# The last unit of a fused recommender kernel: a transpose in halves, three stores on the GpSimd queue, one fused VectorE operation

## The chip, the cores and the metric

The kernel runs on one core of one Trainium2 chip. The metric is device time in microseconds (us), the median over repeated runs. Each kernel also has a profile of one execution, whose span, from the first to the last instruction, is some 2 us shorter than the time (2275.2 of 2277.03 us in the profiled run of the kernel before).

## The reference

Six layers of a cross network on 16384 rows of 1024 features, in bf16:

```python
def reference(x0, ws, bs):
    x = x0                                  # 16384 x 1024
    for l in range(ws.shape[0]):            # 6 layers
        proj = jnp.einsum('bd,de->be', x, ws[l]) + bs[l]
        x = x0 * proj + x
    return x
```

## The kernel before

The kernel works on pairs of blocks of 512 rows, feature by feature on the partitions, so x is transposed. There are 16 pairs and 6 layers, hence 96 units, each a Strassen-like product with four result blocks Q, U, V and W. The last unit has code of its own, because its result must be transposed back and stored while no later work hides it:

- Q (block 11) and U (block 12) go through a DMA transpose on the sync queue and then through a store;
- V (block 22) and W (block 21) are transposed on TensorE against an identity into PSUM, copied to SBUF by ScalarE and VectorE, and stored in halves.

A table of ranks orders the last unit's operations; each engine's queue follows it.

```python
RLAST = {**R0, **ranks("""
...
trQ@19 stQ@24 trU@22.5 stU@26 stVa@27 stVb@27.5 stWa@28 stWb@29
""")}
...
            for m in range(KH):
                ttop(f"Wm{m}", W[:, m, :], W[:, m, :], blk(x0T, 1, 0)[:, m, :], MULT, ...)
            for nm, n in (("Q", 0), ("U", 1)):
                def tr(n=n, xfin=xfin, xo=xo):
                    nc.sync.dma_start_transpose(out=xo[:, 0, n]..., in_=xfin[:, 0, n]...)
                add("tr" + nm, tr, [f"xf{nm}0", f"xf{nm}1"] + XT, [f"xo{nm}"])

                def st(n=n, xo=xo, r0=r0):
                    nc.sync.dma_start(out[r0 + n * NB:r0 + (n + 1) * NB, 0:H]..., xo[:, 0, n]...)
                add("st" + nm, st, [f"xo{nm}"], ["out"])
            for nm, C, bank, n in (("V", V, pX, 1), ("W", W, pA, 0)):
                for m in range(KH):
                    ...                       # transposes on TensorE into PSUM
                    def cp(...):
                        if nm == "V" or m == 3:
                            nc.scalar.copy(out=d, in_=s_)
                        else:
                            nc.vector.tensor_copy(out=d, in_=s_)
```

## Time and profile before

| | kernel before |
|---|---|
| time, median of the first 3 runs | 2277.72 us (2276.81 to 2277.87) |
| TensorE busy | 2265.4 of 2275.2 us |
| last transposing matmul starts | 2269.19 us |
| last copy ends | 2270.08 us |
| last store issued, landed | 2270.16, 2273.92 us |
| end of the span | 2275.25 us |

Issues, ends and landings are single records of the trace; a landing is the last of the 16 semaphore updates of a transfer. The lines themselves stand in the prediction below.

### The profile page before, as it was taken

The page shows a single profiled execution, that of the slowest core. Times are in us where ns is not written, and L with a number is a line of the kernel's source. Part 1 is how long each engine was busy: PE and PEld are TensorE (multiplying, and loading weights), DVE is VectorE, ACT ScalarE, POOL GpSimd, SP SyncE. Part 2 cuts the span into 40 slices and gives each one's busy share as a digit, 9 for nine tenths or more (in the row PEclk, how much of TensorE's full clock was granted, in tenths as well). Part 3 has the DMA queues.
Part 4 walks back from the last instruction along what each step waited for, and adds up shares of the span by engine and source line. Part 5 has one row for each costly group of instructions (what it writes and reads, how often), then busy time and mean ns, then how long its engine had stood idle before and what let it go on. Part 6 is the DMA issues. An engine that isn't in the chain of part 4 may idle for free.

```text
span 2275.2 us, 34978 instructions
## 1 busy us (share of the span) xinstructions
PE 2265.4 (100%) x12951; PEld 1264.0 (56%) x12951; DVE 2079.9 (91%) x2326; ACT 1839.4 (81%) x3228; POOL 22.1 (1%) x43
## 2 busy tenths in 40 slices
PE   9999999999999999999999999999999999999998
PEld 4455555555555555555555555555555555555554
DVE  7999999999999999999999999999999999999997
ACT  5678888888888888888888888888888888888887
POOL 1110000000000000000000000000000000000000
PEclk9999999999999999999999999999999999999999
DMA  9779797796977969779697796978969689696872
GB/s 279 229 270 289 261 242 269 219 301 209 252 257 221 288 217 260 250 226 283 213 274 241 228 283 204 273 245 230 283 200 292 226 232 286 194 303 216 241 240 65
DMA packets 625868, 557.01 MB, mean 245 GB/s; under 512 B 397600, under 2 KB 552224, under 8 KB 625696
## 3 DMA queue, kind: packets, MB, share of 16 engines
q1 hardware_dynamic: 618864, 534.58, 79.1%
q0 software_dynamic: 5184, 18.88, 2.2%
q8 instruction: 101, 1.65, 0.3%
q10 hardware_dynamic: 1648, 1.32, 0.2%
q14 instruction: 71, 0.58, 0.1%
HBM read 436.22 MB, written 52.43 MB: 215 GB/s over the span
## 4 chain that ended last, share of the span: by engine, by line
PE 98%; DVE 1%; SPq 0%; DMA 0%; issue 0%; ACT 0%; DVEq 0%
PE pA L285 57%; PE pX L389 24%; PE pX L285 16%; DVE ev L198 1%; SPq L529 0%; DMA wp<-in_ws_dram 0%; DVE xst L198 0%; DVE T L198 0%; DVE ti L198 0%; DVE wp L198 0%; SPq L538 0%; ACT ev L294 0%; DVE x0T L487 0%; DVEq L608 0%; DVEq L198 0%
## 5 line engine op out<-in xcount | busy, mean ns | idle before, releaser
L285 PEld LDWEIGHTS <-wp 128*128 128x128 bf16 x7904 | 772.3, 98 | 843.7 <-issue 3.9
L285 PE MATMUL pA<-T,wp 128*128 128x512 bf16 x4608 | 1054.9, 379 | 0.5 <-DVE T L198 0.5
L294 ACT ACTIVATE ev<-pA,b_all 128x512 bf16<-128x512 f32 x1124 | 704.8, 690 | 211.8 <-PE pA L285 211.4
L389 PEld LDWEIGHTS <-wp 128*128 128x128 bf16 x4984 | 487.1, 98 | 156.6 <-issue 15.2
L198 DVE TENSOR_TENSOR ev<-ev,x0T 128x2048 bf16<-128x2048 bf16 (+2 forms) x484 | 482.7, 999 | 8.1 <-ACT ev L294 1.5
L198 DVE TENSOR_TENSOR xst<-ev,xst 128x2048 bf16<-128x2048 bf16 x319 | 388.9, 1219 | 18.6 <-DVE ev L198 0.5
L389 PE MATMUL pX<-ti,wp 128*128 128x256 bf16 x2848 | 397.6, 272 | 0.0
L198 DVE TENSOR_TENSOR ev<-ev,ev 128x2048 bf16<-128x2048 bf16 (+1 forms) x283 | 343.7, 1215 | 26.7 <-ACT ev L294 9.8
L294 ACT ACTIVATE ev<-pX,b_all 128x512 bf16<-128x512 f32 x412 | 289.4, 705 | 59.9 <-PE pX L285 49.3
L285 PE MATMUL pX<-xst,wp 128*128 128x512 bf16 x1376 | 336.4, 379 | 0.0
L285 PE MATMUL pA<-xst,wp 128*128 128x512 bf16 x1280 | 313.5, 379 | 0.0
L290 ACT COPY pX<-pA 128x512 f32<-128x512 f32 x412 | 256.3, 625 | 44.7 <-PE pA L285 44.3
L290 ACT CAST ev<-pX 128x512 bf16<-128x512 f32 x384 | 224.8, 619 | 49.0 <-ACT ev L294 37.6
L198 DVE TENSOR_TENSOR ev<-iu,ip 128x1024 bf16<-128x1024 bf16 x178 | 122.4, 688 | 120.7 <-ACT iu L290 120.7
L290 ACT COPY pX<-pX 128x512 f32<-128x512 f32 x356 | 208.7, 587 | 8.4
L290 ACT CAST iu<-pX 128x512 bf16<-128x512 f32 x356 | 196.8, 639 | 0.0
L198 DVE TENSOR_TENSOR T<-xst 128x2048 bf16<-128x2048 bf16 x160 | 194.8, 1217 | 0.3
L198 DVE TENSOR_TENSOR T<-xst,T 128x2048 bf16<-128x2048 bf16 x160 | 194.5, 1216 | 0.0
L389 PE MATMUL pX<-T,wp 128*128 128x256 bf16 x1068 | 160.2, 273 | 0.0
L290 ACT CAST ip<-pX 128x512 bf16<-128x512 f32 x178 | 104.7, 589 | 54.1 <-PE pX L389 54.1
L389 PE MATMUL pX<-xst,wp 128*128 128x256 bf16 x888 | 133.2, 273 | 0.0
L198 DVE TENSOR_TENSOR xst<-ev,x0T 128x2048 bf16<-128x2048 bf16 x64 | 78.2, 1222 | 1.6
(44 smaller groups left out, 624.3 us busy)
## 6 DMA issues: line engine op xcount, KB each, us to landing
wp<-Lc SPq DMA_DIRECT2D x538, 512.0 KB, 4.6
wp<-in_ws_dram SPq DMA_DIRECT2D x285, 512.0 KB, 5.3
out_dram<-x0T SPq DMA_DIRECT2D x30, 1024.0 KB, 8.6
Lc<-wp POOLq DMA_DIRECT2D x24, 512.0 KB, 6.2
Lc<-isum POOLq DMA_DIRECT2D x12, 512.0 KB, 6.9
w<-in_ws_dram SPq DMA_DIRECT2D x5, 512.0 KB, 6.3
wp<-in_ws_dram ACTq DMA_DIRECT2D x2, 512.0 KB, 5.8
out_dram<-x0T SPq DMA_DIRECT2D x2, 512.0 KB, 3.6
```

Source lines behind the costliest of these rows:

```text
L198: nc.vector.tensor_tensor(out=o, in0=a, in1=b, op=op)
L285: nc.tensor.matmul(bank[:], lhsT=wt[(u, w)][:, k, m * P:(m + 1) * P], rhs=rhs[:, k, :], start=(start and k == 0), stop=(k == KH - 1), skip ...
L290: add(name, lambda: nc.scalar.copy(out=dst, in_=src), rd, wr)
L294: add(name, lambda: nc.scalar.activation(out=dst, in_=src, func=IDENT, bias=b_all[:, c:c + 1], scale=1.0), rd, wr)
L389: nc.tensor.matmul(pX[bank][:, m * NQ:(m + 1) * NQ], lhsT=wv[:, k, m * P:(m + 1) * P], rhs=rhs[:, k, :], start=(start and m == 0 and k == ...
```

## The change

Its intent is a shorter tail. The U transpose is cut in two, so that its first half need not wait for the second half of U. The stores of Q and U leave the sync queue, where they stand behind transposes, for the GpSimd queue. The last quarter of W is biased and multiplied in one VectorE operation straight from PSUM, which frees ScalarE of its last activation, and the copies of W are dealt out anew.

```diff
-trQ@19 stQ@24 trU@22.5 stU@26 stVa@27 stVb@27.5 stWa@28 stWb@29
+trQ@19 stQ@20 trU0@20.5 trU1@22.5 stU0@24 stU1@26 stVa@27 stVb@27.5 stWa@28 stWb@29
...
-            biased(f"E4.{m}", W[:, m, :], pA[m][:], 1, m, [A[m]], [f"W.{m}"])
+            if not (last and m == KH - 1):
+                biased(f"E4.{m}", W[:, m, :], pA[m][:], 1, m, [A[m]], [f"W.{m}"])
...
-            for m in range(KH):
+            for m in range(KH - 1):
                 ttop(f"Wm{m}", W[:, m, :], W[:, m, :], blk(x0T, 1, 0)[:, m, :], MULT, ...)
...
+            add("Wm3", lambda c=c, x0T=x0T: nc.vector.scalar_tensor_tensor(
+                out=W[:, KH - 1, :], in0=pA[KH - 1][:], scalar=b_all[:, c:c + 1],
+                in1=blk(x0T, 1, 0)[:, KH - 1, :], op0=ADD, op1=MULT), ...)
+            outs = [("Q", xfin[:, 0, 0], xo[:, 0, 0], 0, 0, H)]
+            outs += [(f"U{h}", xfU[:, h], xoU[:, h], NB, h * HQ, (h + 1) * HQ) for h in range(2)]
+            for nm, src, dst, r, c0, c1 in outs:
+                add("tr" + nm, lambda ...: nc.sync.dma_start_transpose(...), ...)
+                add("st" + nm, lambda ...: nc.gpsimd.dma_start(...), ["xo" + nm], ["out"])
...
-                        if nm == "V" or m == 3:
+                        if nm == "V" or m in (0, 2):
                             nc.scalar.copy(out=d, in_=s_)
```

More of the change, by code (lines that the diff above doesn't have):

```diff
@@ L440 @@
             xfin, xo = quad(xsts[free]), quad(x0Ts[free])
+            halves = lambda t: t[:].rearrange("r n k (j p) -> r (n k j) p", p=P)[:, KH * KH:2 * KH * KH].rearrange(
+                "r (h j k) p -> r h j k p", h=2, j=KH)
+            xfU, xoU = halves(xsts[free]), halves(x0Ts[free])
             XF = [f"xs.{free}.{a}{b}" for a, b in QD]
@@ L455 @@
                 ttop(f"Vx{h}", V[:, sl], V[:, sl], blk(xs, 1, 1)[:, sl], ADD, half("V", h) + [XI[1, 1]], half("V", h))
-                ttop(f"Ux{h}", xfin[:, 0, 1].rearrange("r j k p -> r k j p")[:, sl], v4(U[:])[:, sl],
+                ttop(f"Ux{h}", xfU[:, h].rearrange("r j k p -> r k j p"), v4(U[:])[:, sl],
                      v4(blk(xs, 0, 1))[:, sl], ADD, half("U", h) + [XI[0, 1]] + XF, [f"xfU{h}"])
-            for m in range(KH):
+            for m in range(KH - 1):
                 ttop(f"Wm{m}", W[:, m, :], W[:, m, :], blk(x0T, 1, 0)[:, m, :], MULT, [f"W.{m}", X0[1, 0]], [f"W.{m}"])
-            for nm, n in (("Q", 0), ("U", 1)):
-                def tr(n=n, xfin=xfin, xo=xo):
-                    nc.sync.dma_start_transpose(out=xo[:, 0, n].rearrange("p j k r -> p (j k) r"),
-                                                in_=xfin[:, 0, n].rearrange("r j k p -> r (j k p)"))
-                add("tr" + nm, tr, [f"xf{nm}0", f"xf{nm}1"] + XT, [f"xo{nm}"])
-                def st(n=n, xo=xo, r0=r0):
-                    nc.sync.dma_start(out[r0 + n * NB:r0 + (n + 1) * NB, 0:H].rearrange("(j p) d -> p j d", p=P),
-                                      xo[:, 0, n].rearrange("p j k r -> p j (k r)"))
-                add("st" + nm, st, [f"xo{nm}"], ["out"])
@@ new lines @@
+            c = l * KD + 2 * KH - 1
+            add("Wm3", lambda c=c, x0T=x0T: nc.vector.scalar_tensor_tensor(
+                out=W[:, KH - 1, :], in0=pA[KH - 1][:], scalar=b_all[:, c:c + 1], in1=blk(x0T, 1, 0)[:, KH - 1, :], op0=ADD, op1=MULT),
+                [A[KH - 1], X0[1, 0]], [f"W.{KH - 1}"])
+            outs = [("Q", xfin[:, 0, 0], xo[:, 0, 0], 0, 0, H)]
+            outs += [(f"U{h}", xfU[:, h], xoU[:, h], NB, h * HQ, (h + 1) * HQ) for h in range(2)]
+            for nm, src, dst, r, c0, c1 in outs:
+                add("tr" + nm, lambda src=src, dst=dst: nc.sync.dma_start_transpose(
+                    out=dst.rearrange("p j k r -> p (j k) r"), in_=src.rearrange("r j k p -> r (j k p)")),
+                    (["xfQ0", "xfQ1"] if nm == "Q" else ["xf" + nm]) + XT, ["xo" + nm])
+                add("st" + nm, lambda dst=dst, r=r0 + r, c0=c0, c1=c1: nc.gpsimd.dma_start(
+                    out[r:r + NB, c0:c1].rearrange("(j p) d -> p j d", p=P), dst.rearrange("p j k r -> p j (k r)")),
+                    ["xo" + nm], ["out"])
```

## The prediction

> **What bounds the kernel now.** I read the page first, then the last 20 us of the trace, since the diff touches only the last of 96 units. The head of the page and its chain say that the matmuls bind the whole program:
>
> ```profile
> span 2275.2 us, 34978 instructions
> PE 2265.4 (100%) x12951; PEld 1264.0 (56%) x12951; DVE 2079.9 (91%) x2326; ACT 1839.4 (81%) x3228; POOL 22.1 (1%) x43
> ```
>
> TensorE is busy for 2265.4 of 2275.2 us, and no matmul is removed. So only the few us in which TensorE no longer sets the pace can change. The timeline of the sync engine in the tail (start, length of the issue, both in us) shows the order in which transfers leave:
>
> ```profile
> 2254.48 1.82 SPq L462 DMA_TRANSPOSE x0T<-xst  x1
> ...
> 2262.86 1.32 SPq L462 DMA_TRANSPOSE x0T<-xst  x1
> ...
> 2264.28 1.25 SPq L467 DMA_DIRECT2D out_dram<-x0T  x1
> ...
> 2267.24 0.38 SPq L467 DMA_DIRECT2D out_dram<-x0T  x1
> ...
> 2268.22 0.37 SPq L491 DMA_DIRECT2D out_dram<-x0T  x1
> ...
> 2269.20 0.98 SPq L491 DMA_DIRECT2D out_dram<-x0T  x2
> ```
>
> The first transpose (block 11, "Q") has landed by 2258.94 (the trace's landing record), but its store leaves at 2264.28: it stands on the same queue behind the second transpose (block 12, "U"), which waits for VectorE until 2262.86. The view of DMA activity from 2254 to 2274 (40 slices of 0.5 us, busy tenths, then GB/s) shows what that costs:
>
> ```profile
> DMA  0005999940000000000089999999799999999980
> GB/s 0 0 0 117 214 214 218 203 101 0 0 0 0 0 0 0 0 0 0 0 180 211 215 211 207 351 375 320 240 346 336 294 296 255 286 289 285 292 252 3
> ```
>
> The DMA engines idle from 2258.7 to 2264.3 and are then full until 2273.7. The waits of the sync engine and the two last instructions of the other engines complete the picture:
>
> ```profile
> SPq L608 <- DMA out_dram<-x0T: 3.7, 1, 3.7
> ```
>
> ```profile
> 2269.44 0.58 ACT L485 CAST x0T<-pA 128x512 bf16<-128x512 f32 x1 [0.27 <-PE pA L476]
> 2270.16 0.39 ACTq L491 DMA_DIRECT2D out_dram<-x0T  x1
> ```
>
> Compute ends at 2270.1; the last store is issued at 2270.16 and lands at 2273.92; a fixed closing sequence of 1.3 us follows (2275.2 - 2273.9). The end is therefore a queue of stores, and not the last evictions.
>
> **What the Trainium skill says.** "DMA: Bandwidth & Descriptors", section "Issuing engines are not separate DMA queues": all issuers share 16 DMA engines, and another issuer saves only issue time. The GpSimd queue thus adds no bandwidth; it only removes the wait behind the transpose. The trace agrees that the data share the engines: one store from ScalarE and four from the sync engine land one after another (2270.25, 2271.13, 2272.12, 2273.39, 2273.92).
> The same page, "Latency and other measured facts", puts the first byte at about 1 us for the GpSimd path and 0.6 us for the hardware path. Here the undisturbed GpSimd stores at the start of the program moved their first packet 1.10 to 1.25 us after issue (at 33.86, 68.59, 102.57 and 115.48), and the hardware store issued at 2267.24 about 1.07 us after (2268.3). So the penalty of the GpSimd path is small in this trace when it is undisturbed.
> "SBUF — State Buffer", section "SBUF: two separate sides", warns that VectorE in a 2-port mode keeps GpSimd from writing descriptors. VectorE runs without a pause from 2258.63 to 2270.1, in two-input operations. The trace is ambiguous: the store issued at 115.48 had its first data at 1.14 us under a running VectorE, but others, with loads in flight too, took 3 to 6 us (82.40, 152.06).
> "VectorE: DVE Perf Modes", section "The perf-mode tier table": a two-input operation with a PSUM operand runs at 1x. The trace's PSUM casts of 128x512 take 680 ns on VectorE against 418 ns for the bf16 product that the fused operation replaces.
>
> **The change, part by part.**
> (1) Store of block 11 to the GpSimd queue. It can leave at 2258.97, has data from 2260.1 and is done by about 2261.6, in the idle gap. In the kernel before it moved between 2266.5 and 2268.2; these 1.7 us of DMA time leave the full stretch.
> (2) Block 12 in two halves. VectorE finishes the first half at 2260.09 + 0.69 = 2260.78, so its transpose leaves about 2260.8. A transpose has data 1.47 us after issue (2262.86 to 2264.33) and moves some 213 GB/s: 0.262 MB in 1.23 us, landed about 2263.7. Its store leaves then, from GpSimd, and moves from 2264.8. The second half's transpose still leaves at 2262.86, moves from 2264.3, shares the engines with that store and lands by about 2266.4; its store has data from about 2267.6 and is done at 2268.5 to 2269.5, as 0.262 MB takes 0.9 us at the 290 GB/s of the last stretch.
> (3) The fused last result. One ScalarE activation (687 ns) of the last unit disappears. The built programs' order shows it: ScalarE goes straight from its third W activation to the four V copies. The first copy started at 2267.13, right behind that activation; its transposed input is ready about 2266.75, so the V copies come about 0.38 us earlier, the first V store 0.37 us earlier (2267.85 for 2268.22), the second likewise (2268.80). On VectorE the fused operation replaces 0.42 by 0.68 us, ending about 2268.5 instead of 2268.28.
> (4) Copies shuffled: ScalarE takes W 0 and 2, VectorE W 1 and 3. The pair 0 and 1 is ready at 2269.2, so that store goes about 0.4 us earlier. The last pair is set by TensorE: its last transposing matmul starts at 2269.19 in both kernels, because the V products before it wait for VectorE's last V sum (start 2266.25, unchanged). The last copy (680 ns from about 2269.4) ends at 2270.1, and the last store leaves at 2270.16 as before. **Compute gives nothing at the very end**; the gain is in the queue alone.
>
> The sum: in the kernel before the last four stores (1.05 MB) moved from about 2270.0 to 2273.7, 0.93 us each. Now the first of them has data from 2267.85 + 1.07 = 2268.9, and 4 x 0.93 = 3.7 us gives 2272.6, landed 2272.8: **1.1 us earlier** than 2273.92. A floor is the last store alone: 2270.16 + 1.07 + 0.93 + 0.2 for landing = 2272.4, which would be 1.5 us. If half of the second U store still lies behind 2268.9, 0.45 us are lost. I take 0.95 us.
>
> **The rivals.**
> A. *Late descriptors.* The Q and U stores have runs of 1024 and 512 bytes, 512 runs each, where the GpSimd stores seen so far have 128 runs of 4096 bytes. If the descriptors take in proportion longer, or VectorE keeps GpSimd out, the U stores move after 2269 and compete with the V and W stores. One U half behind the line leaves 1.1 - 0.9 = 0.2 us; both make it 0.7 us slower. For it: the store issued at 82.40 waited 6.0 us for its first packet. Against: that was among loads, while here the engines are idle until the second transpose.
> B. *A slow close of the GpSimd queue.* The drain view of the closing line shows a long one:
>
> ```profile
> L608 POOLq DRAIN  x3: 39/93/9104, 162.2 to 2275.0; - x3
> ```
>
> It begins with the last GpSimd store (162.27) and ends at 171.35, 1.5 us after that store landed (169.84). If it follows the landing, the new last GpSimd store (landed about 2269) ends it at 2270.5, long before 2272.8, and it costs nothing. If it were a fixed 9.1 us from the issue (about 2266.5), it would end at 2275.6 instead of the 2274.4 at which the closing sequence began, and the kernel would be 1.2 us slower. I give that one in ten.
> C. *Nothing visible.* The three runs before spread over 1.06 us (2276.81 to 2277.87), as much as the gain; the profile of one execution could show a shorter tail with equal medians.
>
> **Range and chances.** The mean of the three runs before is 2277.5 (their median is the highest but one); less 0.95 this is 2276.6. The best case, compute-bound, takes another 0.5 off, and noise 0.6: 2275.5. A slow GpSimd queue adds about 1.5: 2278.1. Two per cent is 45 us, some five times the 8.9 us from the end of the last weight matmuls (2266.3) to the end of the span, so nothing in the change can reach it: within 2% at 0.99, and half a per cent for each side.
>
> **What would show it right or wrong.** Part 1: the DMA view has activity between 2260 and 2262, where it was idle. Part 2: two short transposes on the sync engine near 2260.8 and 2262.9. Part 3: the first V copy on ScalarE starts near 2266.75, and the fused operation lasts about 0.68 us. Part 4: the last copy ends at 2270.1 and the last store lands near 2272.8. If the GpSimd stores' packets appear over 3 us after their issue, rival A holds; if a GpSimd drain ends after the last landing, rival B. The prediction is wrong if the span after is not 0.3 to 1.5 us under 2275.2, or if the matmuls before 2254 move, which nothing in the change should do.

## The result, and the profile after

The changed kernel took 2277.16 us (median of 4 runs, 2276.92 to 2278.28), the kernel before 2277.26 us (median of 4 runs, 2276.79 to 2277.87). The ratio is 1.0, with a 95% interval of 0.9983 to 1.0018. Ratios here are the mean time of one kernel's runs over that of the other's in the same rounds, so not quite the ratio of the quoted medians. The medians differ by 0.10 us, where 0.95 us had been expected.

Whole times are a poor ruler for this. The first transpose of the tail starts at 2254.48 us in one trace of the kernel before and at 2255.02 us in another, so 0.54 us come and go ahead of everything that the change touches. I therefore count the tail **from the issue of the first transpose**, and call that time t. On this ruler the kernel before ends at t = 20.77 and the changed one at t = 20.40. So the tail is 0.37 us shorter, but the last store lands at t = 19.50, against 19.44 before. The queue of stores, which was to give everything, gave nothing.

The head of the page after shows no other large change. The matmul count is lower only because 238 records are missing from this trace: the weight loads are all there, and the second trace of the kernel before (c_before) counts 12713 matmuls too.

```profile
span 2275.4 us, 34743 instructions
PE 2253.0 (99%) x12713; PEld 1264.4 (56%) x12951; DVE 2080.4 (91%) x2325; ACT 1841.6 (81%) x3228; POOL 24.5 (1%) x46
```

The sync engine's timeline after (start, length of the issue, then engine, line and operation) has the two short transposes where the prediction put them, t = 6.32 and 8.37, and the V and W stores ahead of their old places:

```profile
2255.04 1.80 SPq L471 DMA_TRANSPOSE x0T<-xst  x1
...
2261.36 1.24 SPq L471 DMA_TRANSPOSE x0T<-xst  x1
...
2263.41 1.78 SPq L471 DMA_TRANSPOSE x0T<-xst  x1
...
2268.42 0.40 SPq L498 DMA_DIRECT2D out_dram<-x0T  x1
```

The GpSimd timeline after is where the plan failed. Its columns are the same; the bracket gives the idle time before and what ended it:

```profile
2262.47 0.77 POOL L474 DMA_DIRECT2D out_dram<-x0T  x1 [2099.52 <-issue]
2264.96 0.77 POOL L474 DMA_DIRECT2D out_dram<-x0T  x1 [1.72 <-issue]
2268.31 0.75 POOL L474 DMA_DIRECT2D out_dram<-x0T  x1 [2.59 <-DMA x0T<-xst]
```

The Q transpose landed at 2259.47, and GpSimd's wait for it ended at 2259.505, but the Q store left at 2262.47: **3.0 us late**. "issue" in the bracket means that the profile knows no releaser. The two U stores each left 0.55 us after their data. The view of DMA activity over the same stretch of both kernels, t = 3 to 20 in 40 slices of 0.425 us, shows what came of it. Before:

```profile
DMA  9800000000000004999999998899999999999500
GB/s 202 165 0 0 0 0 0 0 0 0 0 0 0 0 0 99 216 208 219 210 212 307 376 361 258 280 347 316 336 277 298 233 304 284 290 289 288 163 0 0
```

After:

```profile
DMA  9700000000399799997999700029999799999700
GB/s 201 162 0 0 0 0 19 0 0 0 69 216 208 153 328 328 308 254 153 207 273 319 260 10 0 0 83 258 265 339 290 190 278 284 292 290 283 231 0 0
```

The Q store now moves between t = 8.9 and 11.2, upon the second half transpose, which was issued at t = 8.37 and lands at 12.73. That is when the whole, undivided transpose landed before (12.74). Then the engines idle for some 1.2 us (three slices), and the second U store goes out at t = 13.28, together with the V stores. The last slices, from t = 14.5 on, are as full as before.

The rest is as planned. The first V copy on ScalarE starts at t = 12.28 for 12.65 before, and the fused operation takes 0.74 us (745 ns). ScalarE before:

```profile
2267.13 2.04 ACT L485 CAST x0T<-pX 128x512 bf16<-128x512 f32 x4
```

ScalarE and the fused operation after:

```profile
2267.32 2.05 ACT L492 CAST x0T<-pX 128x512 bf16<-128x512 f32 x4 [0.40 <-PE pX L483]
...
2270.76 0.39 ACTq L498 DMA_DIRECT2D out_dram<-x0T  x1
```

```profile
2268.41 0.74 DVE L465 SCALAR_TENSOR_TENSOR ev<-pA,b_all,x0T 128x512 bf16<-128x512 f32 x1
```

The 0.37 us that the tail did lose come from the closing sequence, which ran from last landing to end in 0.90 us instead of 1.33; the last landing itself came 0.06 us later. In the trace, the sync engine closes by checking the semaphores of all outstanding transfers in a fixed order, one check every 61 ns. Before, the last store to land held the semaphore checked first, so eight checks (2273.94 to 2274.37) followed its landing. In the changed kernel one hardware transfer fewer precedes it in the rotation, the last store holds the semaphore checked last, and no check is left behind it. This is luck, not design.

### The profile page after: what moved, and what is told of

Its sections match the earlier page's. It is cut to its first block, busy times and chain, and to the rows that moved or that the text cites. A ratio compares the mean times of both kernels' runs of the same rounds, so it can differ in the third digit from the quotient of the medians.

```text
span 2275.4 us, 34743 instructions
## 1 busy us (share of the span) xinstructions
PE 2253.0 (99%) x12713; PEld 1264.4 (56%) x12951; DVE 2080.4 (91%) x2325; ACT 1841.6 (81%) x3228; POOL 24.5 (1%) x46
## 3 DMA queue, kind: packets, MB, share of 16 engines
q8 instruction: 101, 1.65, 0.3%
## 4 chain that ended last, share of the span: by engine, by line
PE 98%; DVE 1%; issue 1%; SPq 1%; DMA 0%; ACT 0%; DVEq 0%
PE pA L285 57%; PE pX L389 24%; PE pX L285 16%; SPq L536 0%; DVE ev L198 0%; DMA wp<-in_ws_dram 0%; DVE xst L198 0%; DVE T L198 0%; DVE ti L198 0%; PE pA L483 0%; DVE wp L198 0%; SPq L545 0%; PE pX L483 0%; ACT ev L294 0%; DVE x0T L494 0%
## 5 line engine op out<-in xcount | busy, mean ns | idle before, releaser
L285 PE MATMUL pA<-xst,wp 128*128 128x512 bf16 x1205 | 302.4, 379 | 4.0
```

Source lines behind the costliest of these rows:

```text
L285: nc.tensor.matmul(bank[:], lhsT=wt[(u, w)][:, k, m * P:(m + 1) * P], rhs=rhs[:, k, :], start=(start and k == 0), stop=(k == KH - 1), skip ...
```

## The experiments

Every tail is measured on the same ruler, in us from the issue of the first transpose. The columns are single records of each trace; "closing" is the end of the span less the last landing.

| kernel | Q store leaves | last U transpose lands | last landing | closing | end |
|---|---|---|---|---|---|
| before | 9.80 | 12.74 | 19.44 | 1.33 | 20.77 |
| c_before | 9.79 | 12.71 | 19.40 | 1.35 | 20.75 |
| after | 7.43 | 12.73 | 19.50 | 0.90 | 20.40 |
| c_after | 7.12 | 12.67 | 19.49 | 0.92 | 20.41 |
| e_q_early_sync | 4.37 | 12.65 | 19.30 | 1.33 | 20.62 |
| e_q_gpsimd | 7.15 | 13.26 | 19.94 | 0.98 | 20.92 |
| e_all_sync | 4.37 | 11.46 | 18.53 | 1.22 | 19.75 |
| e_all_sync_unfused | 4.37 | 11.47 | 18.86 | 1.22 | 20.08 |
| e_all_sync_lanes | 4.38 | 11.47 | 18.55 | 0.90 | 19.45 |
| e_q_sync_u_gpsimd | 4.37 | 11.48 | 19.99 | 1.35 | 21.34 |
| e_warm | 5.03 | 11.48 | 18.54 | 0.92 | 19.45 |
| e_pad | 4.95 | 11.54 | 18.53 | 0.92 | 19.45 |

All gave correct results. My theory at the start was that the GpSimd issue path had eaten the gain. The rival was that the queue of stores had never been what sets the end.

**Controls: c_after and c_before.** No edit.

> Control: the changed kernel again, to see how far the tail of one execution repeats. All times of the tail are counted from the issue of the first transpose (t = 0). First run: Q store issued at 7.43, second transpose landed 9.37, third 12.73, last landing 19.50, end of span 20.40; before: last landing 19.44, end 20.77. Every theory expects the same within about 0.1 us for issues that hang on compute, and within 0.2 us for landings. If the last landing moves by over 0.4 us, single traces can't tell the theories apart.

> Control: the kernel before again, for the scatter of the single trace that the tails are compared with. First trace, from the first transpose: second transpose issued 8.38 and landed 12.74, last store issued 15.68, last landing 19.44, end 20.77. Expected within 0.1 us for issues and 0.2 us for landings; if the last landing is off by more, the differences of 0.14 us between kernels are not to be read.

The tails repeat: last landings within 0.04 us, ends within 0.02 us. Only the late Q store scatters (7.43 and 7.12), and the profile names no releaser that would explain by how much. Time of c_after 2277.2 us, of c_before 2277.54 us, one run each.

**e_q_early_sync: the order alone.** One rank of the kernel before:

```diff
-trQ@19 stQ@24 trU@22.5 stU@26 ...
+trQ@19 stQ@20 trU@22.5 stU@26 ...
```

> The kernel before with one rank changed: the Q store stands before the second transpose on the sync queue. Theory 1 (the GpSimd issue path ate the gain: the Q store left 3.0 us after its data and each U store 0.5 us after): the Q store leaves at 4.5, has moved by 7.5, the second transpose is undisturbed, and the last landing comes 0.8 to 1.5 us before that of the kernel before (19.44), so 18.0 to 18.7. Theory 2 (the queue of stores was never what sets the end; the last store's landing is set by its issue and a slow write of 512-byte runs): last landing within 0.2 us of 19.44. Closing sequence as in the kernel before, 1.33 us, because the last store keeps the semaphore that is checked first.

The Q store left at 4.37 and had landed by 7.37, as expected. The last landing, however, came at 19.30, only 0.14 us earlier (0.10 against c_before): a miss for my theory in its first form, and inside the range that the rival had named (within 0.2 us of 19.44). The DMA view of this kernel, t = 3 to 20, says why:

```profile
DMA  9800059990000004999993000999999999999300
GB/s 203 165 0 0 0 188 349 349 328 19 0 0 0 0 0 97 219 207 218 217 209 67 0 0 19 345 340 332 315 286 283 233 314 286 292 283 288 87 0 0
```

Where the Q store moved before (the 22nd to 25th slice, up to 376 GB/s), there is now a gap: the U store can leave only when the U transpose has landed at 12.65, and it has its first data a microsecond later. The Q store had filled a wait, and had hardly delayed anything: the U store landed at 15.68, for 15.77 before. The full DMA engines of the view before were two queues, one behind the other, with a latency between them that the Q store covered. Time 2277.1 us (5 runs, 2276.55 to 2278.44), ratio 0.9998 (0.9986 to 1.0011).

**e_q_gpsimd: the same, with the Q store on GpSimd.** Beside the rank:

```diff
-                    nc.sync.dma_start(out[r0 + n * NB:...
+                    (nc.gpsimd if n == 0 else nc.sync).dma_start(out[r0 + n * NB:...
```

> The same order, but the Q store alone on the GpSimd queue. Theory 1: the Q store again leaves about 3 us late (7.4), its data fall together with the U transpose (issued at 8.38), the transpose lands later than in the kernel before (12.75), and the last landing is between that of the kernel with the early store on the sync queue and 19.4. Theory 2: as e_q_early_sync, 19.4. In both the last store moves to the semaphore checked last, so the closing sequence shortens from 1.33 to about 0.9 us; if it stays at 1.33 the order of the checks is not what shortened it in the changed kernel.

The Q store left at 7.15, 2.8 us after its data, and fell upon the U transpose, which landed at 13.26, 0.5 us later than in the kernel before. The last landing, 19.94, is beyond my range: moving this one store to GpSimd made the tail worse than leaving it behind the transpose. The closing shrank to 0.98 us, here with the last landing on the semaphore checked last but one. Time 2278.35 us, one run.

**e_all_sync: the changed kernel without GpSimd.**

```diff
-                add("st" + nm, lambda ...: nc.gpsimd.dma_start(
+                add("st" + nm, lambda ...: nc.sync.dma_start(
```

> The changed kernel with its three GpSimd stores on the sync queue instead (halves, fused result and copies kept). Theory 1: the Q store leaves at 4.5, the half transposes land at 8.8 and about 11.3, the U stores leave at about 9.7 and 11.4, V stores as in the changed kernel (13.4, 14.4), and the last landing is 1.0 to 1.5 us earlier than 19.50, thus 18.0 to 18.5; the time about 1 us under the kernel before. Theory 2: last landing within 0.2 us of 19.50. Closing: the last store holds the third semaphore checked, so about 1.2 us.

The last landing is 18.53, 0.97 us earlier than after and just short of what I had expected (1.0 to 1.5 us), although the last store leaves at 15.72 in both. The second half transpose lands undisturbed, 3.08 us after its issue (4.36 in the changed kernel). The DMA view, t = 3 to 20, has the Q store alone in its gap, and each later transfer after the other with room between:

```profile
DMA  9800059990299604999950892039899999940000
GB/s 203 169 0 0 0 188 347 349 330 19 64 218 209 126 0 104 216 202 255 294 163 0 252 290 75 0 105 292 227 265 305 265 310 280 290 130 0 0 0 0
```

Time 2276.21 us (5 runs, 2275.76 to 2276.22) against 2277.46 us for the kernel before (9 runs, 2276.68 to 2278.64): all five lie below all nine, though the interval of the ratio, 0.9993 (0.9979 to 1.0007), is wider than that. So the rival falls: the stores did set the end. It is the GpSimd queue that gave the gain back.

**e_all_sync_unfused: what the fused result is worth.** The lines of the change for Wm3 and the copies are undone in e_all_sync.

> All stores on the sync queue and the halves kept, but the last result again biased on ScalarE and multiplied on VectorE, and the copies as in the kernel before. The V and W stores leave at 13.74, 14.72, 15.18, 15.68 as before in place of 13.38, 14.36, 14.85, 15.72. If the queue of stores sets the end, the last landing is 0.3 to 0.4 us later than with the fused result (18.53), about 18.9. If the end hangs on the last store alone, which leaves at the same time either way, it stays at 18.5.

The last landing is 18.86, so the fused operation with the new deal of copies is worth 0.33 us once the queue is clear. Step by step in this order, with all stores on the sync queue: Q early 0.14 (19.44 to 19.30), halves 0.44 (19.30 to 18.86), fused result 0.33 (18.86 to 18.53), together 0.91. In another order the shares could differ; no run tried one. Time 2277.2 us (4 runs).

**e_q_sync_u_gpsimd and e_warm: what makes GpSimd late.** The first puts the Q store alone on the sync queue; the second adds to the changed kernel a small GpSimd store ahead of the Q store (with the rank `warm@12.2` in the table):

```diff
+            warm = dram.tile([P, 64], BF16, name="warm")
+            add("warm", lambda: nc.gpsimd.dma_start(warm[:], T[4][:, 0, 0:64]), ["T4"], [])
```

> The changed kernel with the Q store alone on the sync queue and the two U stores left on GpSimd. Theory 1a (slow restart): now the first U store is the first GpSimd work in 2,100 us, so it leaves some 2.7 us after its data (9.4), near 12.1, the second just behind it near 12.9; the second half transpose lands undisturbed at 11.5; the last landing is near 19.0. Theory 1b with the fixed 0.5 us alone: the U stores leave at 9.9 and 12.0 and the last landing is 18.6, as with all stores on the sync queue (18.53).

> The changed kernel plus one small GpSimd store (128 runs of 128 bytes, to a scratch tensor) that waits for T4, about 2.4 us before the first transpose is issued (t = 0). Theory 1a (the GpSimd queue is slow to restart after 2,090 us without work, and the 3.0 us before the Q store are that restart): the Q store leaves at 4.9 to 5.2 in place of 7.1 to 7.4, lands near 8.5, the second half transpose lands at 11.5 to 12.0 in place of 12.7, the second U store leaves 0.5 us later, and the last landing is 18.6 to 19.1 in place of 19.5. Theory 1b (every GpSimd store behind two waits leaves late, or VectorE at work keeps GpSimd out): the Q store still leaves at 7.1 to 7.4 and the last landing stays at 19.5.

In e_q_sync_u_gpsimd the first U store, now the first GpSimd work for 2,100 us, left at 12.59, 3.2 us after its data, and the last landing was 19.99, worse than the 19.0 I had expected. In e_warm the Q store left at 5.03 and the last landing was 18.54, the same as with all stores on the sync queue. But the small store itself, behind 2,090 us without work, left 0.29 us after VectorE had written T4 (2252.58 to 2252.87). So idleness alone does not make GpSimd late, and the name "slow restart" was wrong. Times 2278.04 and 2276.25 us, one run each.

The instruction packets in the trace's DMA records gave the next theory. In the changed kernel an 8 KB instruction packet moves at 2260.81, between the end of GpSimd's wait and the Q store. The DMA view of 2259.5 to 2262.4, counts by queue, has nothing else in it:

```profile
DMA packets 1, 0.01 MB, mean 3 GB/s; under 512 B 0, under 2 KB 0, under 8 KB 0
...
q14 instruction: 1, 0.01, 0.7%
```

Such a packet stands at the same place in c_after and e_q_gpsimd and ahead of the first U store in e_q_sync_u_gpsimd. In these four traces it moves 1.1 to 1.5 us after the data of the waiting store have landed, and the store leaves 1.65 to 1.73 us after the packet. The kernel before has none there. In e_warm it moved to 166.57 us, a few us after the last weight store. In the kernels whose tail has no GpSimd store, the kernel before among them, a packet of the same queue stands near 175 us instead, some 4 us after the end of GpSimd's drain behind its last weight store (drain to 171.35, packet at 175.69 us in the kernel before).

**e_pad: the fetch without a store.** Eight tiny memsets behind GpSimd's last weight store, 2,090 us before the tail:

```diff
+        if u == 8:
+            pad = const.tile([P, 8], BF16, name="pad")
+            for i in range(8):
+                op(base, lambda i=i: nc.gpsimd.memset(pad[:, i:i + 1], 0.0))
```

> The changed kernel plus eight one-column memsets on GpSimd behind its last weight store, near 165 us, and nothing else; the stores stay on GpSimd. Theory 1c (the 2.7 to 3.0 us before the Q store are a fetch of GpSimd's next block of instructions, which begins only when the wait ends: an 8 KB instruction packet appears between the landing of the Q transpose and the Q store in the changed kernel in all its traces and in e_q_gpsimd, in e_q_sync_u_gpsimd before the first U store, and in e_warm 4 us after the last weight store instead): the memsets move the block's end ahead of the wait, the packet moves to near 167 us, the Q store leaves at 5.0, and the last landing is 18.5 and the end 19.45, as in e_warm. Rival 1d (what e_warm mended was the GpSimd store path itself, which needs a store shortly before): memsets 2,090 us earlier change nothing, Q store at 7.1 to 7.4, last landing 19.5.

It went as theory 1c said. The GpSimd timeline of e_pad, to be read against that of the changed kernel above, where t = 0 is at 2254.73:

```profile
2259.68 0.76 POOL L474 DMA_DIRECT2D out_dram<-x0T  x1 [2096.27 <-DMA x0T<-xst]
2265.03 0.76 POOL L474 DMA_DIRECT2D out_dram<-x0T  x1 [4.59 <-issue]
2266.82 0.75 POOL L474 DMA_DIRECT2D out_dram<-x0T  x1 [1.02 <-DMA x0T<-xst]
```

The Q store leaves 0.59 us after its data landed, and the releaser named is now the transpose. The packet moved too: the DMA view of 163 to 170 us counts one instruction packet in the changed kernel,

```profile
q14 instruction: 1, 0.01, 0.3%
```

and two in e_pad:

```profile
q14 instruction: 2, 0.02, 0.6%
```

Time 2275.89 us (6 runs, 2275.49 to 2276.31) against 2277.98 us (10 runs, 2277.11 to 2278.63); again no run overlaps, ratio 0.9991 (0.9979 to 1.0004). The tail accounts for 1.3 us of the 2.1 us between these medians (20.77 - 19.45); the rest lies outside the tail and is not explained. Eight memsets that compute nothing make the changed kernel do what it was meant to.

**e_all_sync_lanes: the order of the closing checks.** Five tiny stores to a scratch tensor in the middle of the program turn the rotation of semaphores:

```diff
+        if u == NU // 2:
+            lanes = dram.tile([5, P, 64], BF16, name="lanes")
+            for i in range(5):
+                op(base + 23, lambda i=i: nc.sync.dma_start(lanes[i], zeros[:, 0:64]))
```

> All stores on the sync queue, plus five tiny stores to a scratch tensor in the middle of the program, so that the last store takes the semaphore that the closing sequence checks last in place of the third. If the order of the checks is worth time (61 ns each), the closing sequence from last landing to end shrinks from 1.22 to about 0.9 us and the span to 19.45 us after the first transpose; last landing as with all stores on the sync queue, 18.5. If the closing is fixed otherwise, 1.2 stays.

The last landing stayed (18.55), and the closing went from 1.22 to 0.90 us. So the order of the checks is worth what the trace says. Time 2275.99 us (5 runs, 2275.65 to 2276.51), ratio 0.9992 (0.9979 to 1.0004). This kernel and e_pad end at the same t, 19.45, ahead of both the kernel before (20.77) and the changed one (20.40). No run of theirs is as slow as the fastest run of the kernel before in the same rounds (2277.11), but the intervals of both ratios reach past 1, so whole times alone do not settle the gain.

## Why the prediction was right or wrong

The time fell in the stated range, at 2277.16 us, but that was luck rather than insight: the range, 2275.5 to 2278.1, also holds the time of the kernel before. By the prediction's own test (a span 0.3 to 1.5 us under 2275.2) it was wrong: the span was 2275.4. The scatter ahead of the tail added 0.56 us and the shorter closing took 0.43 off; the planned gain is missing, step by step:

- **What bounds the kernel: half right.** The end is a queue of stores; e_all_sync shows it. But the step "these 1.7 us of DMA time leave the full stretch" failed. The stretch was not one queue: the Q store lay in the wait between the U transpose and the U store, and taking it out moved the last landing by 0.14 us (e_q_early_sync), although 1.7 us of transfer had left. The view showed full engines; it does not show which transfer anybody is waiting for.
- **Part 1, "It can leave at 2258.97": failed.** On the prediction's clock the Q store left at 2261.91, 2.9 us later. A delay ahead of the issue was not among the rivals. Of the 3.0 us behind its wait, e_pad takes away all but 0.6; what the memsets remove, by the reading above the fetch, is thus 2.2 to 2.4 us (c_after's delay from landing to issue, 2.76, and after's, 2.99, less 0.59).
- **Part 2: the first half right, the second wrong.** The first half transpose left at t = 6.32 and landed at 9.37, both within 0.2 us. The second was to land by t = 11.9 and its store to be done by 15.0 at the latest; they came at 12.73 and 16.78, because the late Q store moved beside the transpose. Without it (e_pad) they come at 11.54 and 14.87. So halves are worth 0.44 us with the stores on the sync queue, and they were cancelled here by the neighbour.
- **Part 3: right.** The V copies came 0.37 us earlier and the two V stores 0.36 each (the prediction's 2268.80 for the second would have been 0.40). The fused operation took 745 ns, not 680: the prediction had taken the time of a PSUM cast, another operation, for it. The fused result with the new copies is worth 0.33 us where the queue is clear; what it gave in the changed kernel no run shows.
- **Part 4: right.** The last store left at t = 15.72 for 15.68.
- **The sum.** A last landing at 2272.8 is t = 18.3. Where the issues come on time, it is 18.53 (e_pad, e_all_sync). So 1.1 us was the size of the plan, 0.91 its measure, and 0 what the changed kernel got.
- **"A fixed closing sequence of 1.3 us": wrong.** It was 0.90 in the changed kernel, and that is the whole of its shorter tail.
- **Rival A** named the outcome, one U half behind the line, for a wrong reason. The late part was the issue: the Q store's first packet came 1.47 us after it, 1.34 in e_pad, not over 3. The prediction also misread VectorE's last stretch: from 2268.20 on its operations are copies, not two-input ones. In e_pad VectorE is as busy and the GpSimd stores leave and land normally: 3.59 us from issue to landing for 0.5 MB (3.00 on the sync queue), 2.73 and 2.79 for halves (2.47 and 2.28). **Rival B** fell: the GpSimd drain after its last store ended at 2273.46, 1.6 us after that store landed and 1.1 us before the last landing. **Rival C** was closest on the medians.

What stays open: the 0.5 to 0.6 us between a landing and a GpSimd issue, also in e_pad, which no run varied; and which engine's block each instruction packet holds, which the records do not say. That the packet belongs to GpSimd is inferred from its moving with eight GpSimd instructions; that those eight remove the delay is shown.

## What to carry to other kernels

A DMA view that is full does not tell what the end waits for: before moving a transfer, find who waits for it, or whether it only fills somebody's latency. An engine that sleeps through a long program may have to fetch its next instructions when its wait ends; let it pass that point earlier, or put late, urgent transfers on a queue that has been running. When a change is worth a microsecond in two thousand, measure the tail from an event of its own, because the whole time moves more than that by itself.

## What the Trainium skill lacked or had wrong

- "Runtime: NRT & Kernel Launch", section "Instruction fetch mechanics", says that an engine fetches its next page while it executes the current one, and that the cost is mostly hidden. It lacks the case of an engine parked on a wait at the end of its page: there 2.2 to 2.4 us came after the wait, on the path, in two traces of the changed kernel, and eight memsets placed earlier removed them (Q store 2.76 and 2.99 us after its data, 0.59 in e_pad). That this is a fetch is the reading of the packets above. The section speaks of 16 KiB blocks; the packet seen here has 8192 bytes, as have all 71 instruction packets of its queue in the changed kernel's trace, while the 101 of another queue have 16384.
- "DMA: Bandwidth & Descriptors", section "Issuing engines are not separate DMA queues", holds as far as bandwidth goes, but says that only the time to initiate is at stake. The same store took 0.59 to 2.99 us from its data to its issue on GpSimd, against 0.02 us on the sync queue (e_all_sync), and in e_q_gpsimd the last landing was 0.50 us later than in the kernel before for it.
- No page that I read has the order of the closing semaphore checks: 61 ns each, and 0.3 to 0.4 us by the place of the last transfer (1.22 to 0.90 us in e_all_sync_lanes).
